# Attention scores over 64 rows instead of 32, odd heads joined by DMA, and a third buffer for VectorE's exponentials

## The chip, the core and the metric

The kernel runs on one core of a Trainium2 chip. A core has five engines that run side by side and meet only at semaphores: TensorE (PE, matrix products into PSUM), ScalarE (ACT, table functions such as the exponential), VectorE (DVE, elementwise work), GpSimd (POOL, used here for a few small jobs) and SyncE (SP, which issues nearly all DMAs of this kernel, strictly in the order in which they were written down). The metric is the time of one execution in device microseconds.

## What is computed

The reference normalises the input and runs two branches on it, an attention block and a token-mixing MLP, and adds both to the input:

```python
xn = _layernorm(x)                       # 2048 tokens x 512
q, k, v = split(xn @ wqkv)               # 32 heads of 16 columns each
p = softmax(q @ k.T * 16 ** -0.5)        # 32 heads x 2048 x 2048
A = (p @ v).reshape(2048, 512) @ wo
u = gelu(layernorm(xn).T @ w1 + b1)      # 512 x 1376, over tokens
B = (u @ w2 + b2).T                      # 2048 x 512
out = x + A + B
```

The softmax dominates: 32 x 2048 x 2048 exponentials. A head has only 16 columns, so a score product uses 16 of the 128 rows of the PE array.

## The kernel before

**Blocks.** Queries are cut into 4 groups of 512 (`qb`). The 32 heads lie in 4 groups of 8 (`T`), and each group is taken in two halves, `e_ = 0` (even heads) and `e_ = 1` (odd heads). A block `b` is one `qb`, one `T` and one `e_`: four heads (`r = 0..3`), 512 queries, all 2048 keys. There are 32 blocks, and each has 16 key tiles `kt` of 128 keys.

**Scores** (`score_mm`, L619). In the transposed keys `KT` and queries `QT`, head `2r` of a group lies on rows 32r to 32r+15 and head `2r+1` on rows 32r+16 to 32r+31. Keys are kept whole. For queries there are two copies per `qb` and `T`, one with the odd heads' rows set to zero and one with the even heads' rows set to zero, made by one VectorE product with a mask (L1032). So a score matmul runs over 32 rows, 16 of which contribute nothing. Two such matmuls (a pair, 128 keys x 512 queries each, into two PSUM banks) are one unit of work. The first pair of a key tile has heads 0 and 1 (rows 0 to 63), the second heads 2 and 3 (rows 64 to 127). Three bank pairs of PSUM rotate.

**Exponentials.** A pair goes either to ScalarE (one `activation`, L696, into a buffer `pT`) or, for up to four key tiles of a block (`D_KTS`), to VectorE, which builds the exponential from bit operations: L880 once per pair out of PSUM, then L899, L906, L912 and L919 once per key tile over all four heads. A key tile treated like this is called a group here. Its intermediate results have two buffers (`dbuf`).

**Weighted values** (`pv_round`, L726). Four matmuls of 128 rows and 32 columns add p times V for four heads into one PSUM bank, head r on partitions 32r to 32r+31: rows 0 to 15 are the result, row 16 is the softmax denominator (V carries a column of ones). A ScalarE tile needs one such round, a VectorE group three.

**End of a block** (`epilogue`). VectorE copies the bank to `OT32` (L811); SP issues four small DMAs that gather the denominators (`rl`), VectorE inverts them (L827), SP puts them to DRAM and spreads them over the partitions again (`denb`); POOL multiplies (L846) into `oT`, which has one slab per block. As odd heads also come out on rows 0 to 15 of their strips, the output weight `wo` is kept in a padded form, `wo_pad`, with eight slabs of 128 rows, half of them zeros, and the output product takes eight matmuls per 128 tokens (L1178, L1205).

**The order.** All instructions are placed by a small planner inside the kernel (`Dispatch`) that runs once when the program is built: it holds an estimated duration for each kind of work (`EST`), steps a clock of its own, and gives every engine its instructions in the order that comes out. On the chip each engine then follows its list in that order and waits at semaphores. The MLP and the projections are filled in as `extras` between scores. The planner also keeps a running sum of PE work over 3.41 us (`GATE_US`) and adds products with a zero matrix (`keep_warm`, L1013) when the sum falls below `GATE_AIM`; a score pair counts as 0.5 in that sum, a full matmul of 512 columns as 1.

## Time and profile before

| what | value |
|---|---|
| median of three runs | 846.33 us (841.46, 846.33, 846.75) |
| the profiled execution | 852.81 us, span 851.0 us |
| mean granted PE clock in the span | 0.954 |
| exponentials on ScalarE | 842 pairs, 783.4 us busy |
| groups on VectorE | 91 (182 pairs) |
| first exponential on ScalarE starts | 14.86 us |
| last one has ended | 839.0 us |

The times are of whole executions; the profile is of one execution, some 6 us longer than the median, and 1.8 us of it lie outside the span. In a line of the profile, the number after `x` is how many instructions the group has, then come busy time and mean duration, and then the engine's idle time just before them with what ended it. Matmul ends are modelled, so a PE that reads as busy may still be running at half speed; the granted clock tells that.

### The profile page before, as it was taken

To read this page: it belongs to the slowest core of one execution; us is meant where nothing else is said; L and a number is where in the kernel's file an instruction comes from. 1 tells how busy PE (TensorE), PEld (TensorE's weight loads), DVE (VectorE), ACT (ScalarE), POOL (GpSimd) and SP (SyncE) were. 2 spreads that over 40 slices of the span, in tenths; PEclk is the share of its full clock that TensorE was granted. 3 is DMA by queue.
4 is the path that set the end of the run, shared out by engine and by line. 5 is a ranking of instruction groups with operands and counts; after the bars stand their busy time and mean duration, and the time that the engine had idled before them with its cause. 6 is when DMAs were issued, how large, how long until landed. Compare 5 with 4: busy or idle time off the path is not lost.

```text
span 851.0 us, 14650 instructions
## 1 busy us (share of the span) xinstructions
PE 783.6 (92%) x6084; PEld 222.4 (26%) x6084; DVE 723.7 (85%) x874; ACT 792.4 (93%) x863; POOL 80.7 (9%) x112
## 2 busy tenths in 40 slices
PE   5999799999999999999999999899899999999995
PEld 3433232222222222222222222212222222222221
DVE  6678788899999899988998989749678999899885
ACT  5999699999999999999999999969889999999994
POOL 5234000000000000000000010000000001000000
PEclk9999799999999999989999999959889999999996
DMA  7100000001111111111001111111020111110000
GB/s 197 27 15 18 22 14 14 8 8 39 40 39 39 39 27 39 38 32 44 22 11 43 43 42 44 43 30 35 21 66 16 25 40 44 43 43 14 15 14 25
DMA packets 75698, 29.25 MB, mean 34 GB/s; under 512 B 63472, under 2 KB 71664, under 8 KB 75632
## 3 DMA queue, kind: packets, MB, share of 16 engines
q1 hardware_dynamic: 72464, 26.75, 12.8%
q10 hardware_dynamic: 3168, 1.57, 0.7%
q8 instruction: 47, 0.77, 0.4%
q14 instruction: 19, 0.16, 0.1%
HBM read 25.70 MB, written 2.35 MB: 33 GB/s over the span
## 4 chain that ended last, share of the span: by engine, by line
ACT 40%; PE 31%; DVE 21%; DMA 3%; SPq 2%; issue 2%; POOL 1%; ACTq 0%; DVEq 0%
ACT pT L696 39%; PE ps L619 12%; PE ps L726 8%; DVE xreg L880 7%; DVE big L906 3%; PE ps L1013 3%; DVE big L912 3%; DVE big L899 2%; DMA rl<-OT 2%; PE ps L1173 2%; DVE xreg L919 2%; SPq L394 1%; PE ps L1178 1%; PE ps L1102 1%; PE ps L1024 1%
## 5 line engine op out<-in xcount | busy, mean ns | idle before, releaser
L696 ACT ACTIVATE pT<-ps 128x1024 bf16<-128x1024 f32 x842 | 783.4, 1114 | 38.0 <-PE ps L619 32.8
L619 PE MATMUL ps<-QT,KT 32*128 32x512 bf16 x2048 | 349.7, 395 | 43.9 <-ACT pT L696 21.8
L880 DVE TENSOR_SCALAR xreg<-ps 128x1024 int16<-128x1024 f32 x182 | 222.2, 1221 | 58.6 <-PE ps L619 57.1
L619 PEld LDWEIGHTS ps<-QT,KT 32*128 32x128 bf16 x2048 | 85.9, 91 | 363.6 <-ACT pT L696 233.6
L726 PE MATMUL ps<-pT,V 128*32 128x512 bf16 x1684 | 160.4, 401 | 2.9 <-DVE V L493 1.5
L906 DVE TENSOR_TENSOR big<-xreg,big 128x2048 bf16<-128x2048 bf16 x91 | 115.9, 1274 | 1.5
L912 DVE TENSOR_TENSOR big<-big 128x2048 bf16<-128x2048 bf16 x91 | 115.3, 1267 | 1.8
L1013 PE MATMUL ps<-xnT,zero 128*128 128x512 bf16 x272 | 83.0, 392 | 0.8 <-DVE OT L811 0.6
L846 POOL TENSOR_TENSOR oT<-OT,denb 128x512 bf16<-128x512 f32 x23 | 35.5, 1545 | 504.5 <-DMA denb<-den_scr 460.3
L899 DVE TENSOR_SCALAR big<-xreg 128x2048 int16<-128x2048 int16 x91 | 66.6, 732 | 1.6
L919 DVE TENSOR_SCALAR xreg<-xreg 128x2048 int16<-128x2048 int16 x91 | 65.5, 720 | 0.0
L726 PE MATMUL ps<-xreg,V 128*32 128x512 bf16 x728 | 58.2, 392 | 4.3 <-DVE xreg L919 4.1
L726 PEld LDWEIGHTS ps<-pT,V 128*32 128x32 bf16 x1684 | 37.8, 95 | 88.9 <-issue 77.4
L1173 PE MATMUL ps<-gT,w2blk 128*128 128x512 bf16 (+1 forms) x176 | 55.4, 392 | 0.2
L1102 PE MATMUL ps<-big,w1blk 128*128 128x512 bf16 (+1 forms) x176 | 53.7, 388 | 0.0
L726 PE MATMUL ps<-big,VS 128*32 128x512 bf16 x364 | 36.1, 387 | 0.0
L846 POOL TENSOR_TENSOR big<-OT,denb 128x512 bf16<-128x512 f32 x8 | 12.6, 1572 | 197.0 <-DMA denb<-den_scr 146.2
L827 DVE RECIPROCAL rl<-rl 128x16 f32<-128x16 f32 x31 | 7.7, 249 | 23.1 <-DMA rl<-OT 23.0
L811 DVE COPY OT<-ps 128x512 f32<-128x512 f32 x31 | 21.2, 685 | 5.1 <-PE ps L726 4.9
L1013 PEld LDWEIGHTS ps<-xnT,zero 128*128 128x128 bf16 x272 | 16.9, 98 | 32.7 <-issue 27.1
L522 PE MATMUL ps<-wqkv_sb,xnT 128*128 128x128 bf16 x256 | 24.6, 227 | 0.0
L726 PEld LDWEIGHTS ps<-xreg,V 128*32 128x32 bf16 x728 | 16.0, 97 | 25.0 <-issue 11.2
(75 smaller groups left out, 365.0 us busy)
## 6 DMA issues: line engine op xcount, KB each, us to landing
denb<-den_scr SPq DMA_DIRECT2D x124, 64.0 KB, 2.0
w1blk<-in_B_w_dram SPq DMA_DIRECT2D x10, 512.0 KB, 4.1
w2blk<-in_B_w_dram SPq DMA_DIRECT2D x16, 320.0 KB, 3.4
big<-in_A_x_dram SPq DMA_DIRECT2D x16, 128.0 KB, 2.1
out_dram<-osb SPq DMA_DIRECT2D x16, 128.0 KB, 1.8
rl<-OT SPq DMA_DIRECT2D x124, 2.0 KB, 1.8
xreg<-in_A_x_dram SPq DMA_DIRECT2D x3, 512.0 KB, 9.0
wqkv_sb<-in_A_wqkv_dram ACTq DMA_DIRECT2D x3, 384.0 KB, 9.9
```

Source lines behind the costliest of these rows:

```text
L619: sc.add("pe", lambda e: e.matmul(bank(bk), lhsT=KT[32 * r:32 * r + 32, T, 128 * kt:128 * (kt + 1)], rhs=QT[32 * r:32 * r + 32, sl, :], st ...
L696: sc.add("act", lambda e: e.activation(pT[:, buf, :], ps[:, s_ * 1024:(s_ + 1) * 1024], ACTF.Exp, scale=EXP_SCALE), reads=[("bank", 2 * s_ ...
L726: sc.add("pe", lambda e, r=r, lhs=lhs, rhs=rhs: e.matmul(bank(PV_BANK)[32 * r:32 * r + 32, :], lhsT=lhs, rhs=rhs, start=first, stop=last, ...
L846: sc.add("pool", lambda e: e.tensor_tensor(oT(qb)[:, G, :], OT32[:, eb, :], denb[:, :], ALU.mult), reads=[("OT32", eb)] + [("denb", r) for ...
L880: sc.add("dve", lambda e: e.tensor_scalar(bv_i[:, i, 1024 * hf:1024 * (hf + 1)], ps[:, s_ * 1024:(s_ + 1) * 1024], EXP_BIAS, 0.0, ALU.add, ...
L899: sc.add("dve", lambda e: e.tensor_scalar(ge_i[:, 0, :], bv_i[:, i, :], 0x7F, 0x3F80, ALU.bitwise_and, ALU.bitwise_or), reads=[("bD", i)], ...
L906: sc.add("dve", lambda e: e.tensor_tensor(ge_f[:, 1 + i, :], bv_f[:, i, :], ge_f[:, 0, :], ALU.mult), reads=[("bD", i), ("gD",)], writes=[ ...
L912: sc.add("dve", lambda e: e.tensor_tensor(ge_f[:, 1 + i, :], ge_f[:, 1 + i, :], ge_f[:, 0, :], ALU.mult), reads=[("eD", i), ("gD",)], writ ...
L919: sc.add("dve", lambda e: e.tensor_scalar(bv_i[:, 2 + i, :], bv_i[:, i, :], 0x7F80, None, ALU.bitwise_and), reads=[("bD", i)], writes=[("v ...
L1013: sc.add("pe", lambda e: e.matmul(bank(PV_BANK), lhsT=zero[:, :], rhs=xnT[:, 0, 0:512], start=first, stop=first), reads=[("zero",)] + [("x ...
L1102: mms = [lambda st=st: sc.add("pe", lambda e: e.matmul(bank(EX_BANK)[0:m, :], lhsT=w1blk[:, slot, st, 0:m], rhs=h_sb[:, st, :], start=(st ...
L1173: mms.append(lambda ft=ft, m=m: sc.add("pe", lambda e: e.matmul(bank(EX_BANK), lhsT=w2blk[0:m, slot, ft, :], rhs=gT[0:m, ft, :], start=(ft ...
```

## The change

1. **Scores over 64 rows.** `QT` has eight slabs instead of four: for each block two versions, and version `r % 2` holds only the 16 rows of heads r = 0 and 2 (or 1 and 3), zeros elsewhere. A score matmul reads 64 rows (0 to 63 or 64 to 127). A pair now has heads r and r+2, so that its two matmuls lie in the two halves of the array. The zero rows are written once by POOL; the 16-row strips come by DMA. VectorE scales the projected queries once into `qst` (512 columns instead of 1024), and SP issues eight DMAs per group of heads (`qt_spread`). The planner counts a score pair as 1.0 (`S_WORK`).
2. **Odd heads on rows 16 to 31.** For odd heads the slice of V starts 16 columns earlier, so that results come out on rows 16 to 31 of the strip and the denominator on row 15. POOL multiplies an odd block into `oTe`, and four DMAs copy its rows 16 to 31 into the even block's slab of `oT`. `wo` needs no padding any more: four matmuls instead of eight per 128 tokens. For the very last block a small padded copy, `wo_last`, remains.
3. **A third buffer** for VectorE's groups (`NDB = 3`, extra space `dmore`).
4. **Planner.** `GATE_AIM` 8.0 to 6.5, with a second test over 0.6 of the stretch; `HOLD_SLACK` 0.3 to 0.2; the gather of denominators is expected to take 3.6 instead of 2.6; POOL's product is put beside a VectorE instruction that reads PSUM (`beside`): it waits for the VectorE instruction ahead of that one, or starts without it after 4 us.
5. Small: the residual rows `xr` move into `w1blk`; padding of V and VS and its memsets go.

```diff
+NDB = 3
-HOLD_SLACK = 0.3
+HOLD_SLACK = 0.2
-GATE_AIM = 8.0
+GATE_AIM = 6.5
+GATE_AIM_SHORT = 6.0
+S_WORK = 1.0
+BESIDE_US = 4.0
...
-        return sum(w for _, w in self.recent) < GATE_AIM
+        if sum(w for _, w in self.recent) < GATE_AIM:
+            return True
+        return sum(w for q, w in self.recent if q >= self.t - 0.6 * GATE_US) < 0.6 * GATE_AIM_SHORT
...
+            sc.add("act", lambda e: e.activation(qst[:, :], bank(EX_BANK), ACTF.Identity, scale=QSCALE),
+                   reads=[("bank", EX_BANK)], writes=[("qst",)])
+            qt_spread(1, 1)
+
+        def qt_spread(sl, e_):
+            for r in range(4):
+                q = 32 * r + 16 * e_
+                dma("sp", QT[q:q + 16, 2 * sl + r % 2, :], qst[q:q + 16, :], reads=[("qst",)],
+                    writes=[("QT", sl, r % 2)], name="qt_spread")
...
-                bank(bk), lhsT=KT[32 * r:32 * r + 32, T, 128 * kt:128 * (kt + 1)],
-                rhs=QT[32 * r:32 * r + 32, sl, :], start=True, stop=True,
-                tile_position=(32 * r, 0)),
+                bank(bk), lhsT=KT[64 * (r // 2):64 * (r // 2) + 64, T, 128 * kt:128 * (kt + 1)],
+                rhs=QT[64 * (r // 2):64 * (r // 2) + 64, 2 * sl + r % 2, :], start=True, stop=True,
+                tile_position=(64 * (r // 2), 0)),
...
-                for r in (2 * hf, 2 * hf + 1):
-                    score_mm(b, kt, r, 2 * s_ + r % 2)
+                for r in (hf, hf + 2):
+                    score_mm(b, kt, r, 2 * s_ + r // 2)
...
-                            return (k * H + 8 * T + 2 * r + e_) * 17
+                            return (k * H + 8 * T + 2 * r + e_) * 17 - 16 * e_
...
-                at[("rl", b)] = dp.use("sp", 4 * EST["sp"]) + EST["dma"]
+                at[("rl", b)] = dp.use("sp", 4 * EST["sp"]) + EST["dma_rl"]
...
+            def mult(after=()):
+                dst = oTe[:, :] if e_ else oT(qb)[:, T, :]
+                keys = [("oTe",)] if e_ else [oT_key(qb, T, 0), oT_key(qb, T, 1)]
...
+            if e_:
+                def put_odd():
+                    for r in range(4):
+                        q = 32 * r + 16
+                        dma("sp", oT(qb)[q:q + 16, T, :], oTe[q:q + 16, :], reads=[("oTe",)],
+                            writes=[oT_key(qb, T, 1)], name="ot_odd")
...
+                if beside and dp.free["pool"] <= dp.t:
+                    beside.pop(0)[1]((sc.streams["dve"][-1],))
...
-                sc.add("dve", lambda e: e.tensor_tensor(
-                    QT[:, 2 * i:2 * i + 2, :], bank(EX_BANK).unsqueeze(1).broadcast_to([128, 2, 512]),
-                    qmask[:, :].unsqueeze(2).broadcast_to([128, 2, 512]), ALU.mult),
+                sc.add("dve", lambda e: e.tensor_scalar(qst[:, :], bank(EX_BANK), QSCALE, None, ALU.mult),
+                       reads=[("bank", EX_BANK)], writes=[("qst",)])
...
+            def go():
+                qt_spread(2 * i, 0)
+                qt_spread(2 * i + 1, 1)
...
-            ng = 0 if lastqb else NG
+            ng = 0 if lastqb else 4
...
-            ng = NG - 2
+            ng = 3
```

## The prediction

> **What bounds the kernel now.** I read the busy shares and the 40 slices first. ScalarE is busy 93% of the span, PE 92%, VectorE 85%; in the row of the granted PE clock some slices fall below 9.

> ```profile
> PE 783.6 (92%) x6084; PEld 222.4 (26%) x6084; DVE 723.7 (85%) x874; ACT 792.4 (93%) x863; POOL 80.7 (9%) x112
> ...
> PEclk9999799999999999989999999959889999999996
> ...
> L696 ACT ACTIVATE pT<-ps 128x1024 bf16<-128x1024 f32 x842 | 783.4, 1114 | 38.0 <-PE ps L619 32.8
> L619 PE MATMUL ps<-QT,KT 32*128 32x512 bf16 x2048 | 349.7, 395 | 43.9 <-ACT pT L696 21.8
> ...
> L1013 PE MATMUL ps<-xnT,zero 128*128 128x512 bf16 x272 | 83.0, 392 | 0.8 <-DVE OT L811 0.6
> ```

> An exponential costs 783.4/842 = 0.930 us of ScalarE. To see where its 58.6 idle us lie I asked for the busy time in stretches (span, PE, PEld, DVE, ACT, POOL, then the clock):

> ```profile
> 80.00:100.00 20.00, 15.15 (x100) 4.28 (x98) 14.11 (x18) 13.30 (x15) 3.34 (x2) 0.66 0.14 41
> 560.00:580.00 20.00, 20.00 (x105) 3.90 (x105) 9.03 (x11) 14.33 (x16) 0.00 (x0) 0.62 0.18 46
> 600.00:620.00 20.00, 17.61 (x125) 4.04 (x125) 15.93 (x18) 15.62 (x17) 1.96 (x1) 0.83 0.05 15
> ...
> 100.00:360.00 260.00, 246.75 (x1984) 69.94 (x1984) 237.55 (x260) 256.99 (x283) 14.73 (x10) 1.00 0.12 28
> ```

> At full clock ScalarE is busy 256.99 of 260 us, 19.77 in 20: it is the bound. In the eight slices of 20 us with a fallen clock (from 80, 360, 380, 540, 560, 600, 620 and 820) it is busy 132.7 us instead of 8 x 19.77 = 158.2. **The clock drops cost 25.5 us.** Start and tail take most of the other idle time.

> **What makes the clock fall.** Followed in steps of 3.41 us, the clock is 1.00 or 0.50, and every change falls on one grid of 3.41 us. Three windows of that grid, the first two followed by a drop, the third not:

> ```profile
> 551.45:554.86 3.41, 2.20 (x20) 0.60 (x16) 3.41 (x3) 3.41 (x5) 0.57 (x1) 1.00 0.00 0
> 599.24:602.65 3.41, 1.32 (x20) 0.37 (x16) 1.85 (x3) 1.91 (x3) 0.00 (x0) 1.00 0.04 3
> 766.49:769.90 3.41, 2.97 (x20) 0.69 (x17) 3.20 (x5) 3.23 (x4) 0.00 (x0) 1.00 0.00 0
> ```

> **What empties those windows** the timelines around the drops show. At 551 POOL's product runs beside VectorE, whose 1.22 us product takes 2.18; the score pair that needs the bank waits, and PE with it:

> ```profile
> 550.27 1.75 POOL L846 TENSOR_TENSOR big<-OT,denb 128x512 bf16<-128x512 f32 x1 [24.36 <-DMA denb<-den_scr]
> 550.93 2.18 DVE L906 TENSOR_TENSOR big<-xreg,big 128x2048 bf16<-128x2048 bf16 x1
> 551.59 0.40 PE L619 MATMUL ps<-QT,KT 32*128 32x512 bf16 x4
> 554.30 0.39 PE L619 MATMUL ps<-QT,KT 32*128 32x512 bf16 x2 [0.65 <-DVE xreg L880]
> ```

> The drops at 377 and 835 look the same. At 603 and 630 a reciprocal stands in VectorE's list before its gather has landed, as SP was still busy with a weight load:

> ```profile
> 591.60 4.61 SPq L395 DMA_DIRECT2D w2blk<-in_B_w_dram  x2
> 596.25 0.43 SPq L395 DMA_DIRECT2D big<-in_A_x_dram  x1
> 596.72 2.41 SPq L394 DMA_DIRECT2D rl<-OT  x4
> 600.31 0.25 DVE L827 RECIPROCAL rl<-rl 128x16 f32<-128x16 f32 x1 [4.95 <-DMA rl<-OT]
> ```

> **The change part by part**, against the span of 851.0 us.

> *Scores over 64 rows.* The same 2048 matmuls of 512 columns. A steady window of 3.41 us has about 9 scores and 12 value matmuls: 0.14 + 0.19 = 0.33 of the array before, 0.28 + 0.19 = 0.47 after, above the limit without any filler. PE's two built lists, with time laid along the score pairs at the trace's pace (0.92 us each in the first 128, 0.79 later), agree: 7.7% of windows of 3.41 us lie under 0.37 before, 2.5% after. I keep that third of the loss: -25.5 + 8.2 = **-17.3 us**. Bounds: 0 (the stalls empty PE whatever the weights) to -25.5.

> *PE's time.* The new list has 74 zero matmuls instead of 272 and 60 fewer with `wo`: -258 x 0.215 = -55 us. Five more groups add ten rounds, +2. What is lost is the overlap of one pair's rows 0 to 63 with the next pair's 64 to 127: the four scores above ran in 0.40 us, where two pairs one after the other show 0.61. The old list has 288 such places, of which 81 started together: +17 us, bounds 0 and 288 x 0.215 = 62. Net -36 us (+9 at worst), worth nothing by itself, as ScalarE has 1.2% of idle time in clean stretches. The trace has no 64-row matmul; the nearest row is the 32-row pair, two side by side in 0.39.

> [...]

> *Ten exponentials fewer on ScalarE.* The new list has 832 pairs there and 96 groups on VectorE: -10 x 0.930 = **-9.3 us**. VectorE gets 5 x (2 x 1.221 + 0.732 + 1.274 + 1.267 + 0.720) = 32.2 us. It loses 15 x (1.216 - 0.69) = 7.9 with the queries' evacuation, and, if POOL's product lies beside L880 as planned, the stretching: the four long operations average 1274, 1267, 732 and 720 ns where undisturbed ones show 1224, 1224, 690 and 685, 91 x 0.165 = 15 us. So 733 us in a span near 823, 89%: cover enough, since stretches with 95% run at full ScalarE speed. If POOL starts elsewhere, the 15 us come back on VectorE; in clean stretches ScalarE hardly feels them, but one more drop costs it 2 to 9 us (the slices above).

> *Start.* ScalarE writes `qst` before its first exponential, and must wait for VectorE's read of that bank, which ends at 15.23; 0.69 us for `qst` and 0.27 for a key copy follow, so the first exponential comes near 16.3 instead of 14.86: **+1.5**. POOL's memset of 3072 columns at 1.93/2192 a column is 2.7 instead of 1.9 us; its successors wait for the input's DMA (landed at 8.89) anyway, 0 to +0.5, taken as 0.

> *SP.* New are 124 strips of queries and 60 strips of odd heads. Strips with one buffer key wait for each other's landing; 1.8 to 2.0 us is the nearest rows' time to landing (`rl`, `denb`). A spread of eight then holds SP for 2 x (1.9 + 0.8) = 5.4 us, a join of four for 3 x 1.9 + 0.4 = 6.1: 11.5 per two blocks of some 26 us each, where SP now idles over half the time. Queued behind them are gathers, puts and weight loads; only a late gather is felt, by VectorE's reciprocal. Between copy and reciprocal VectorE's new list holds 4.0 to 6.3 us of work (median 4.9; before 1.4 to 6.4, median 3.8), and a gather on time needs 2.41 + 1.8 = 4.2. In SP's list, loads or a spread stand close ahead of the gathers of blocks 20 to 23 and 25: 2.6, 3.2, 2.2, 5.8 and 0.6 us late, 14 us of VectorE's idle time against the 23.0 that its waits show now. Taken as -2 on ScalarE; bounds -5 and +45, all joins and spreads half in the way. Query strips have half a block, 13 us, before their first use.

> *The rest* (third buffer, `xr`, one evacuation fewer per key) changes no count on ScalarE: 0. The tail keeps its steps, 12 us from the last exponential.

> **Sum:** 851.0 - 17.3 - 9.3 + 1.5 - 2 = 824 us of span, with the 1.8 outside **825.5 us**. That is 2.5% under the median of 846.33, though 3.2% under the execution it is made against; the median runs may have lost some 6 us less to the clock.

> **Rivals.** (1) *The drops stay*, because stalls make them, not thin windows: -9.3 + 1.5 gives 843 + 1.8 = 845, no change. For it: five of seven drops stand behind a named stall. Against: the same stalls elsewhere left no drop where filler stood beside. 0.15. (2) *Slower: SP's list.* If the strips land in 4 us instead of 1.9 (the longest gather took 4.9), a join holds SP for 12 us and a spread for 10; from the point where 20 of the 31 gathers come 3 us late or more, VectorE idles 60 us in order, PE's fixed list waits behind it, and the 1.2% of slack is gone: 825 + 60 less the 14 counted, 870. 0.08. (3) *Zero rows don't count for the clock*, while the filler is gone: 21% of the new list's windows would be under the limit instead of 7.7%, 25.5 x 21/7.7 = 70 us of loss, 851 - 9.3 + 1.5 + 44 + 1.8 = 889. Against: the zero matrices of L1013 do count in the fit. 0.04. (4) *64-row halves don't run side by side*: 1024 x 0.215 = 220 us more PE, then the bound, over 900. 0.02. Better than 812 (no drop left, fewer stalls): 0.05. The forecast, 812 to 836: 0.66.

> **Numbers.** A measurement of this kernel tells about 1% from no change (838 to 855). Faster: 0.66 + 0.05 + 0.02 of the first rival = 0.73; same 0.13; slower 0.14. A range of 808 to 846 holds 0.8.

> **What would show it.** Right: a clock near 0.98 with two or three drops, 832 exponentials at 0.93 us, L906 and L912 near 1230 ns, score pairs at 0.39. Wrong: long VectorE idle times ended by the gather's DMA, joins of over 6 us on SP, scores of two pairs at 0.43 apart, or as many slices of fallen clock as before.

## The result and the profile after

The changed kernel takes 839.32 us (median of 20 runs, 836.08 to 843.60), the kernel before, measured beside it, 850.61 us (20 runs, 841.46 to 857.07). The ratio is 0.9892, with a 95% interval of 0.9867 to 0.9916: **1.1% faster, where 2.5% were forecast.** The profiled execution after took 837.79 us, with a span of 835.7 us and a mean granted PE clock of 0.984 (before 0.954). Executions of one kernel differ in their mean granted clock (0.947 to 0.980 before, 0.976 to 0.986 after): the ratios here leave out the longest ones, medians in us count all, and the profiled execution of the kernel before (852.81 us, clock 0.954, where most others of it have 0.96 to 0.98) is one of the longer, so the two profiles differ by 15.3 us where the ratio stands for 9.

From the page of the kernel after, the busy line, the row of the granted clock and three of the costliest groups (line, engine, operation, tiles and shapes, count | busy us, mean ns | idle us just before them, with what ended most of it):

```profile
PE 734.9 (88%) x5866; PEld 212.3 (25%) x5866; DVE 730.1 (87%) x900; ACT 783.0 (94%) x854; POOL 74.1 (9%) x110
...
PEclk9999999999999999999989999999999999999998
...
L720 ACT ACTIVATE pT<-ps 128x1024 bf16<-128x1024 f32 x832 | 773.3, 1151 | 29.9 <-PE ps L643 25.8
L643 PE MATMUL ps<-QT,KT 64*128 64x512 bf16 x2048 | 367.6, 388 | 68.9 <-ACT pT L720 29.9
...
L1059 PE MATMUL ps<-xnT,zero 128*128 128x512 bf16 x74 | 21.8, 388 | 0.2 <-ACT KT L506 0.2
```

L720 is the old L696, L643 the old L619, L1059 the old L1013. The stretches that had a fallen clock before, and the clean one (stretch, length, then busy time and instructions of PE, PEld, DVE, ACT and POOL, then the clock, the DMA share and GB/s), of the kernel after:

```profile
80.00:100.00 20.00, 18.10 (x164) 6.23 (x164) 19.33 (x23) 20.00 (x23) 1.26 (x1) 1.00 0.07 18
560.00:580.00 20.00, 15.92 (x128) 4.36 (x127) 16.17 (x18) 17.73 (x21) 1.86 (x1) 1.00 0.10 23
600.00:620.00 20.00, 17.97 (x145) 4.94 (x148) 17.25 (x20) 19.58 (x22) 0.00 (x0) 1.00 0.21 48
100.00:360.00 260.00, 238.91 (x1916) 66.94 (x1912) 240.07 (x272) 253.22 (x278) 13.51 (x10) 0.99 0.15 32
```

The clock is back: counted in steps of 3.41 us, it was at half speed for 79.7 us before and is for 29.5 us now, in six single steps and the tail. But look at the last line: between 100 and 360 us ScalarE is busy 253.22 us, **less** than the 256.99 us before, and only 1.4 us of that are lost in a half-speed step (at 262 us); in the second line it lacks 2 us at a full clock. Something new holds it up.

The span can be closed on ScalarE alone, from the group lines and the start of the first exponential:

| us | before | after | change | forecast |
|---|---|---|---|---|
| exponentials (842, 832) | 783.4 | 773.3 | -10.1 | -9.3 |
| its waits ahead of them | 38.0 | 29.9 | -8.1 | -19.3 (clock -17.3, SP -2) |
| first exponential starts | 14.86 | 17.09 | +2.2 | +1.5 |
| span | 851.0 | 835.7 | -15.3 | -27 |

The first three changes add up to -16.0, so hardly anything is left over. Eleven of the missing twelve microseconds are waits of ScalarE. Summed over the half-speed steps between its first and last exponential, ScalarE is idle for 66.6 - 44.8 = 21.8 us before and 20.5 - 13.1 = 7.4 us after. So its waits inside the drops fell by 14.4 us (forecast 17.3), and its waits outside them rose from 16.2 to 22.5 us, by 6.3, where a fall of 2 was forecast.

**What the waits are.** The whole timeline of all engines around 515 us, of the kernel after (start, length, engine, line, operation, tiles, count; in brackets the idle time before it and what ended it; SPq is SP's queue of DMA issues, a run of equal issues being one piece):

```profile
509.63 4.08 SPq L416 DMA_DIRECT2D w2blk<-in_B_w_dram  x2
...
513.76 0.43 SPq L416 DMA_DIRECT2D w1blk<-in_A_x_dram  x1
...
514.23 6.07 SPq L416 DMA_DIRECT2D QT<-qst  x8
...
517.98 0.39 PE L643 MATMUL ps<-QT,KT 64*128 64x512 bf16 x2 [3.01 <-DMA QT<-qst]
...
518.41 1.22 DVE L926 TENSOR_SCALAR xreg<-ps 128x1024 int16<-128x1024 f32 x1 [2.97 <-PE ps L643]
```

SP is in a weight load for 4.08 us, so the eight query strips start only at 514.23. The next block's first score needs strips r = 0 and r = 2. The second was issued only when the first had landed, so PE stands idle for 3.01 us, VectorE for 2.97. The 3.41 us grid shows the price:

```profile
514.99:518.40 3.41, 0.42 (x6) 0.23 (x6) 0.45 (x1) 2.01 (x3) 0.00 (x0) 1.00 0.19 53
518.40:521.81 3.41, 3.41 (x20) 0.65 (x20) 3.37 (x3) 1.88 (x2) 0.00 (x0) 0.50 0.11 22
521.81:525.22 3.41, 3.41 (x46) 0.98 (x38) 1.60 (x3) 3.37 (x5) 0.00 (x0) 1.00 0.28 61
```

The emptied window is followed by one at clock 0.50, and ScalarE loses about 1.4 us in each of the two. The same chain (weight load of 4.00 us, spread of 5.94, PE waiting 2.10) stands before the drop at 723. The join of odd heads does the same to the output product, once:

```profile
792.33 5.87 SPq L416 DMA_DIRECT2D oT<-oTe  x4
...
799.47 0.39 PE L1255 MATMUL ps<-wo_sb,oT 128*128 128x512 bf16 x1 [2.15 <-DMA oT<-oTe]
```

Most other stalls end at SP as well: VectorE's reciprocal waits 2.3 to 3.7 us for a late gather at 260, 413, 563 and 588 us, and three of these lead to a drop in the next window. The gather at 260 was issued behind a join that had held SP for 7.51 us, the other three behind a weight load. Of the six drops only the one at 429.7 stands behind no wait on SP: there POOL's product of 1.27 us (from 423.12) lies beside a VectorE product that takes 2.30 us instead of 1.22, and PE then waits 1.18 us for VectorE. SP's own waits in the kernel after (engine, line, what for: us in total, times, longest) say what holds it, beside waits for inputs that it would have in any order:

```profile
SPq L416 <- DMA w2blk<-in_B_w_dram: 51.2, 16, 3.5
...
SPq L416 <- DMA oT<-oTe: 47.5, 33, 2.9
...
SPq L416 <- DMA QT<-qst: 24.2, 36, 2.3
```

In all three SP waits for a DMA that it has issued itself, whose bytes the next DMA doesn't touch. The kernel tracks dependencies by buffer keys; the two strips of a slab of `QT`, the four strips of odd heads in one slab of `oT`, and the two parts of one load of `w2blk` each share a key, so the later write waits for the earlier one's landing. The first two are new, the third (49.6 us) was there before.

### The profile page after: what moved, and what is told of

Its sections match the earlier page's. It is cut to its first block, busy times and chain, and to the rows that moved or that the text cites. A ratio compares the mean times of both kernels' runs of the same rounds, so it can differ in the third digit from the quotient of the medians.

```text
span 835.7 us, 14448 instructions
## 1 busy us (share of the span) xinstructions
PE 734.9 (88%) x5866; PEld 212.3 (25%) x5866; DVE 730.1 (87%) x900; ACT 783.0 (94%) x854; POOL 74.1 (9%) x110
## 4 chain that ended last, share of the span: by engine, by line
ACT 45%; PE 25%; DVE 17%; DMA 8%; SPq 2%; issue 2%; POOL 1%; ACTq 0%; DVEq 0%
ACT pT L720 45%; PE ps L643 11%; DVE xreg L926 8%; PE ps L744 7%; PE ps L1152 3%; PE ps L1223 2%; DMA w2blk<-in_B_w_dram 2%; DVE big L952 2%; DMA QT<-qst 2%; DMA oT<-oTe 2%; DVE big L958 2%; DMA rl<-OT 1%; SPq L415 1%; DVE big L945 1%; SPq L416 1%
## 5 line engine op out<-in xcount | busy, mean ns | idle before, releaser
L720 ACT ACTIVATE pT<-ps 128x1024 bf16<-128x1024 f32 x832 | 773.3, 1151 | 29.9 <-PE ps L643 25.8
L643 PE MATMUL ps<-QT,KT 64*128 64x512 bf16 x2048 | 367.6, 388 | 68.9 <-ACT pT L720 29.9
L926 DVE TENSOR_SCALAR xreg<-ps 128x1024 int16<-128x1024 f32 x192 | 234.7, 1223 | 61.0 <-PE ps L643 55.9
L643 PEld LDWEIGHTS ps<-QT,KT 64*128 64x128 bf16 x2048 | 90.1, 93 | 359.8 <-ACT pT L720 218.5
L744 PE MATMUL ps<-xreg,V 128*32 128x512 bf16 x512 | 46.7, 395 | 0.8 <-DVE xreg L965 0.8
L876 POOL TENSOR_TENSOR oTe<-OT,denb 128x512 bf16<-128x512 f32 x15 | 19.0, 1268 | 302.2 <-DVE big L958 151.9
L876 POOL TENSOR_TENSOR oT<-OT,denb 128x512 bf16<-128x512 f32 x12 | 17.8, 1482 | 296.8 <-DMA denb<-den_scr 274.0
L965 DVE TENSOR_SCALAR dmore<-xreg 128x2048 int16<-128x2048 int16 x64 | 43.7, 683 | 0.0
L744 PE MATMUL ps<-dmore,V 128*32 128x512 bf16 x256 | 26.0, 396 | 7.2 <-DVE dmore L965 7.2
L965 DVE TENSOR_SCALAR xreg<-xreg 128x2048 int16<-128x2048 int16 x32 | 22.1, 692 | 0.0
L1059 PE MATMUL ps<-xnT,zero 128*128 128x512 bf16 x74 | 21.8, 388 | 0.2 <-ACT KT L506 0.2
L849 DVE RECIPROCAL rl<-rl 128x16 f32<-128x16 f32 x31 | 7.6, 246 | 14.9 <-DMA rl<-OT 14.9
## 6 DMA issues: line engine op xcount, KB each, us to landing
xreg<-in_A_x_dram SPq DMA_DIRECT2D x3, 512.0 KB, 10.1
```

Of the source, the lines that this page charges most:

```text
L643: sc.add("pe", lambda e: e.matmul(bank(bk), lhsT=KT[64 * (r // 2):64 * (r // 2) + 64, T, 128 * kt:128 * (kt + 1)], rhs=QT[64 * (r // 2):64 ...
L720: sc.add("act", lambda e: e.activation(pT[:, buf, :], ps[:, s_ * 1024:(s_ + 1) * 1024], ACTF.Exp, scale=EXP_SCALE), reads=[("bank", 2 * s_ ...
L744: sc.add("pe", lambda e, r=r, lhs=lhs, rhs=rhs: e.matmul(bank(PV_BANK)[32 * r:32 * r + 32, :], lhsT=lhs, rhs=rhs, start=first, stop=last, ...
L876: sc.add("pool", lambda e: e.tensor_tensor(dst, OT32[:, eb, :], denb[:, :], ALU.mult), reads=[("OT32", eb)] + [("denb", r) for r in range(4)],
L926: sc.add("dve", lambda e: e.tensor_scalar(bv_i[:, i, 1024 * hf:1024 * (hf + 1)], ps[:, s_ * 1024:(s_ + 1) * 1024], EXP_BIAS, 0.0, ALU.add, ...
L965: sc.add("dve", lambda e: e.tensor_scalar(vp_i(i), bv_i[:, i, :], 0x7F80, None, ALU.bitwise_and), reads=[("bD", i)], writes=[("vD", i)] + ...
```

## The experiments

Each ratio is against the kernel before, measured beside it on the same chip; the before's median there was 843.6 to 847.9 us. "Waits" is the idle time ahead of ScalarE's exponentials in the profiled execution (38.0 before, 29.9 after).

### The SP queue: a key for each strip

```diff
-writes=[("QT", sl, r % 2)], name="qt_spread"
+writes=[("QT", sl, r % 2, r)], name="qt_spread"
-writes=[oT_key(qb, T, 1)], name="ot_odd"
+writes=[oT_key(qb, T, 1 + r)], name="ot_odd"
```

Each score matmul reads only its own strip's key; the readers of `oT` list all five. The order on every engine is that of the changed kernel.

> The changed kernel with a buffer key of its own for each strip of queries and for each strip of odd heads, so that SP no longer waits for one strip's landing before it issues the next; every engine's order stays. Theory 'SP's list': in the changed kernel's trace, ScalarE loses some 25 us around waits that end with SP (query strips landing late 6.7 us on PE, gathers 14.9 us on VectorE, a join 2.2 us). A spread then holds SP for 8 x 0.45 = 3.6 instead of 6.0 us, a join for 4 x 0.5 = 2.0 instead of 5.9: 825 to 831 us, the clock's drops 2 or 3 instead of 7. Rival 'planned order': the stalls come from the order itself, SP is merely the last to be late: within 3 us of the changed kernel's 839. Rival 'clock': drops as before in number, time within 3 us of 839.

**826.15 us, ratio 0.9759 (0.969 to 0.9829).** That is 11 us below the changed kernel by the ratios, 13 by the medians, 11.7 by the spans (824.0 against 835.7). Waits fell from 29.9 to 21.0. The timeline of this kernel at the same block change:

```profile
507.11 4.96 SPq L416 DMA_DIRECT2D QT<-qst  x8
...
510.13 0.39 PE L643 MATMUL ps<-QT,KT 64*128 64x512 bf16 x1 [0.62 <-DMA QT<-qst]
...
516.26 0.61 PE L643 MATMUL ps<-QT,KT 64*128 64x512 bf16 x4
```

A spread now holds SP for 4.96 us instead of 6.07. More important, PE waits 0.62 us instead of 3.01: strip 2 no longer starts behind strip 0's landing. All PE's waits for strips fall from 6.7 us to 2.8.

The two halves of this edit alone, first the queries, then the joins:

> The changed kernel with keys of their own for the query strips alone (joins of odd heads as in the changed kernel). Theory 'spreads': the query strips are what SP is held by at the wrong place (6.0 us each, 15 times; PE waited 6.7 us for them, and gathers and puts queue behind them): 827 to 832 us. Rival 'joins': 837 to 840 us, and the gain is in the other half.

**830.80 us, ratio 0.9835 (0.9776 to 0.9893)**, waits 25.0.

> The changed kernel with keys of their own for the strips of the odd heads' joins alone. Theory 'spreads': 834 to 839 us, as a join stands after its block's gather and mostly has 10 us of room, but for the wait of 2.2 us at 799. Rival 'joins': 827 to 831 us.

**833.49 us, ratio 0.9869 (0.98 to 0.9939)**, waits 23.9. Their waits lie 4.9 and 6.0 us under the changed kernel's 29.9, and above the 21.0 of both halves together. By the ratios the queries' half is some 5 us faster than the changed kernel and the joins' half 2, both inside the intervals: how the 11 to 13 us divide is not settled.

### The weight load with the same fault

```diff
-reads=[], writes=[("w2blk", slot)], name="ld_w2b"
+reads=[], writes=[("w2blkb", slot)], name="ld_w2b"
```

The product with the last part of `w2` reads the new key. Done on top of the previous kernel, and alone on the kernel before:

> The kernel of e1_own_keys, and in addition the two parts of each weight load w2 have a key of their own, so that SP doesn't wait 3.4 us for the landing of the first before it issues the second; same order. Theory 'SP's list': three of the five long VectorE waits left (gathers 3 to 4 us late at 409, 555 and 582) stand behind such a load; they go, and the clock's drops with them: 815 to 821 us. Rival 'DMA shared': the gather's landing, not its issue, is late, since the weight load of 320 KB moves at the same time: within 3 us of 826.

**809.81 us, ratio 0.958 (0.9525 to 0.9636): the fastest kernel of this study, 4.2% under the kernel before.** Its costliest group and SP's timeline, of this kernel:

```profile
L720 ACT ACTIVATE pT<-ps 128x1024 bf16<-128x1024 f32 x832 | 769.2, 1171 | 6.7 <-PE ps L643 3.4
```

```profile
498.95 1.18 SPq L416 DMA_DIRECT2D w2blk<-in_B_w_dram  x2
500.19 0.42 SPq L416 DMA_DIRECT2D w1blk<-in_A_x_dram  x1
500.65 4.97 SPq L416 DMA_DIRECT2D QT<-qst  x8
...
532.07 2.43 SPq L416 DMA_DIRECT2D big<-oTe  x4
```

The weight load holds SP for 1.18 us instead of 4.08, a join 2.43 instead of 5.87. The waits ahead of exponentials are 6.7 us, the clock is 0.996 and falls only in the tail; VectorE waits 2.7 us in all for gathers (12.7 with the strips' keys alone).

> The kernel before with the two parts of each weight load w2 on keys of their own; same order. Theory 'SP's list': the waits of 4.95 and 2.24 us ahead of VectorE's reciprocal go, and with them the drops at 603 and 630: 6 to 12 us under the kernel before. Rival 'DMA shared': no change, within 3 us.

**834.49 us, ratio 0.9895 (0.9812 to 0.9978).** On the kernel before, this one key is worth 9 us (2 to 16 by the interval), about as much as the whole change brought. On top of the strips' keys it was worth 15 to 16.

### What the rows are worth, and what the lost overlap costs

First the changed kernel with its scores on the head's own 32 rows (the zero rows left out of the product, the same result):

```diff
-lhsT=KT[64 * (r // 2):64 * (r // 2) + 64, ...], tile_position=(64 * (r // 2), 0)
+lhsT=KT[32 * r:32 * r + 32, ...], tile_position=(32 * r, 0)
```

> The changed kernel, same order, but each score matmul runs over its own 32 rows only (the zero strips are left out; the result is the same). Theory 'area': the clock goes by the share of the array in use, so without the doubled rows a fifth of the windows of 3.41 us come under the limit: mean clock under 0.90, 870 to 910 us. Rival 'stalls alone': the rows don't count for the clock, it falls where PE is held up; mean clock about 0.98, 839 us within 4. Rival 'overlap': rows of neighbouring pairs now differ (0 and 64 against 32 and 96), so that neighbouring pairs run together again, and PE gains up to 50 us of slack: 833 to 838.

**880.54 us (four executions, 864.13 to 893.86), ratio 1.0255 (1.012 to 1.039).** The clock row and costliest group of this kernel, in an execution of 888.41 us:

```profile
PEclk9599997896999998899889898799888959879975
...
L720 ACT ACTIVATE pT<-ps 128x1024 bf16<-128x1024 f32 x832 | 780.8, 1114 | 71.5 <-PE ps L643 65.6
```

In the new order, with 74 filler products instead of 272, the zero rows are worth 31 us by the ratios. Nothing but the rows differs; their new place would, by the author's estimate, let neighbouring pairs overlap again, as in the kernel before (four scores in 0.40 us at 551), which speaks for the 32 rows and doesn't make up for the clock. The clock is at half speed for 221.7 us in this execution instead of 29.5; in the shortest, of 864.13 us, its mean of 0.910 stands for an estimated 155 us (twice 0.090 of the span). So rows of zeros count for the clock here (mean 0.984 with them, 0.876 without, in the profiled executions), which agrees with the author's estimate that it goes by the share of the array in use.

Then the kernel before with 64 rows in the scores, its order and filler kept:

```diff
-lhsT=KT[32 * r:32 * r + 32, ...], tile_position=(32 * r, 0)
+lhsT=KT[64 * (r % 2):64 * (r % 2) + 64, ...], tile_position=(64 * (r % 2), 0)
```

> The kernel before, same order and same filler, but each score matmul runs over 64 rows (0 to 63 for heads 0 and 2, 64 to 127 for heads 1 and 3); the scores then add up two heads' products and the values are not the reference's, only the work is of the same size. Theory 'area': a steady window rises by 0.14 of the array, nearly all drops go: mean clock 0.99, 851 - 20 = 828 to 834 us. Rival 'stalls alone': drops stay as they are, 850 us within 4. Rival 'lost overlap': neighbouring pairs no longer run together, 81 x 0.215 = 17 us of PE time come back, and eat part of it: 836 to 845.

**843.68 us, ratio 0.9984 (0.9945 to 1.0023): no measurable change**, although the clock rose to 0.989. The rows bring the clock and take something else. The next kernel takes that alone: 32 rows as before, but the second pair of a key tile in the same rows as the first, so that neighbouring pairs can't overlap.

```diff
-lhsT=KT[32 * r:32 * r + 32, ...], tile_position=(32 * r, 0)
+lhsT=KT[32 * (r % 2):32 * (r % 2) + 32, ...], tile_position=(32 * (r % 2), 0)
```

> The kernel before, same order, still 32 rows a score, but heads 2 and 3 use the rows of heads 0 and 1 (their own keys and queries are left out, so the values are not the reference's), so that a pair can no longer run beside the pair before it. Theory 'overlap has a price': 81 places x 0.215 = 17 us more PE time; some windows get thinner at their ends, 3 to 10 us over the kernel before. That would explain why 64 rows in the order before took away the drops and gave only some 4 us. Rival 'slack': PE has room, within 3 us of the kernel before.

**861.60 us, ratio 1.0165 (1.008 to 1.0251): the lost overlap costs 14 us** (7 to 21 by the interval; 3 to 10 were expected). PE is busy with scores for 373.0 us, before for 349.7. The two groups, of the kernel with 32 rows and no overlap, and of the kernel before with 64 rows:

```profile
L696 ACT ACTIVATE pT<-ps 128x1024 bf16<-128x1024 f32 x842 | 785.8, 1088 | 41.2 <-PE ps L619 35.1
```

```profile
L696 ACT ACTIVATE pT<-ps 128x1024 bf16<-128x1024 f32 x842 | 784.8, 1087 | 24.7 <-PE ps L619 18.1
```

These two have the same order, filler and lack of overlap, and differ in the rows alone: waits fall by 16.5 us, half-clock time from 80.2 us to two short drops and the tail, and the time by 15 us (ratios). That is about the forecast's -17.3, in the order before and with the overlap gone on both sides.

### POOL's wait, the start, the third buffer

The changed kernel, and then the fastest one, without POOL's wait for a VectorE instruction:

```diff
-beside.pop(0)[1]((sc.streams["dve"][-1],))
+beside.pop(0)[1]()
```

> The changed kernel, same order, but POOL's product no longer waits for the VectorE instruction ahead of the one that reads PSUM: it starts as soon as its own inputs are there. Theory 'port': products again fall beside VectorE's long SBUF operations; their stretching goes from about 8 us in the changed kernel to 15 to 20 us, the time up by 2 to 8 us, one or two drops more. Rival 'no matter': the wait only moves POOL's product, ScalarE has other causes to wait: within 2 us of 839.

> The kernel of e5_own_keys_w2 without POOL's wait for the VectorE instruction ahead, as in e4_pool_no_wait. Theory 'port': VectorE's long operations are stretched by some 8 us more in all, 2 to 6 us slower, 812 to 816. Rival 'no matter': within 2 us of 809.8, as in e4_pool_no_wait.

**835.16 us, ratio 0.9868 (0.9791 to 0.9945), and 812.73 us, 0.9598 (0.955 to 0.9646): no difference from the kernels with the wait** (0.9892 and 0.958). The wait does shift POOL's work. The two long VectorE products, after and without the wait:

```profile
L952 DVE TENSOR_TENSOR big<-xreg,big 128x2048 bf16<-128x2048 bf16 x96 | 120.0, 1250 | 0.2
L958 DVE TENSOR_TENSOR big<-big 128x2048 bf16<-128x2048 bf16 x96 | 118.3, 1233 | 1.9
```

```profile
L958 DVE TENSOR_TENSOR big<-big 128x2048 bf16<-128x2048 bf16 x96 | 122.3, 1274 | 1.9
L952 DVE TENSOR_TENSOR big<-xreg,big 128x2048 bf16<-128x2048 bf16 x96 | 121.5, 1266 | 0.2
```

Without the wait VectorE is stretched by some 5.5 us more in these two lines (96 x 16 ns and 96 x 41 ns). The time shows none of it.

The start, in the fastest kernel, with `qst` written by VectorE instead of ScalarE:

```diff
-sc.add("act", lambda e: e.activation(qst[:, :], bank(EX_BANK), ACTF.Identity, scale=QSCALE),
+sc.add("dve", lambda e: e.tensor_scalar(qst[:, :], bank(EX_BANK), QSCALE, None, ALU.mult),
```

> The kernel of e5_own_keys_w2 with the first scaled copy of the queries (qst) written by VectorE instead of ScalarE at the start, so that ScalarE doesn't wait for VectorE's read of the bank before its first exponential. Theory 'start': the first exponential comes 1.3 to 1.5 us earlier (15.0 instead of 16.4), the whole 1 to 1.5 us faster: 808.5. Rival 'hidden': the first scores set it, no change.

**812.55 us, ratio 0.9579 (0.9523 to 0.9634): no gain in time.** The first exponential starts at 16.37 us, against 16.35 with ScalarE's copy. But the two profiled executions didn't reach this point at the same time. ScalarE's first copy of the queries and its first exponential, of the fastest kernel and then of the one with VectorE's `qst`:

```profile
14.12 0.69 ACT L564 ACTIVATE QT<-ps,qmask 128x512 bf16<-128x512 f32 x1 [0.21 <-PE ps L558]
...
16.35 3.03 ACT L720 ACTIVATE pT<-ps 128x1024 bf16<-128x1024 f32 x3
```

```profile
15.20 0.69 ACT L564 ACTIVATE QT<-ps,qmask 128x512 bf16<-128x512 f32 x1 [0.17 <-PE ps L558]
...
16.37 1.02 ACT L720 ACTIVATE pT<-ps 128x1024 bf16<-128x1024 f32 x1 [0.32 <-PE ps L643]
```

From the one to the other it is 2.23 us with ScalarE's `qst` and 1.17 with VectorE's, as in the kernel before (13.69 to 14.86). So the edit does take away 1.06 us, but everything ahead ran 1.08 us later in that execution, where VectorE waited 1.48 us for a part of the input (0.60 in the other). A gain of 1 us is below what four executions of 807.25 to 813.84 us can show.

Two buffers instead of three, in the fastest kernel (`NDB = 2`; the planner then makes another order, with 846 exponentials on ScalarE and 89 groups on VectorE):

> The kernel of e5_own_keys_w2 with two buffers for VectorE's groups instead of three; the planner then gives VectorE fewer groups, and the order differs. Theory 'third buffer lets VectorE take more': 7 groups fewer on VectorE, 14 pairs more on ScalarE, 14 x 0.93 = 13 us slower, 820 to 826. Rival 'count unimportant': within 4 us of 809.8.

**823.48 us, ratio 0.9719 (0.9672 to 0.9765)**, 10.9 us over the 812.55 of the kernel with VectorE's start, which ran on the same chip. The costliest group of the kernel with two buffers:

```profile
L720 ACT ACTIVATE pT<-ps 128x1024 bf16<-128x1024 f32 x846 | 782.7, 1180 | 7.6 <-PE ps L643 5.9
```

Waits are as low as with three buffers (7.6 against 6.7); the difference is 782.7 - 769.2 = 13.5 us of exponentials. Once little else holds ScalarE, most of what a pair costs there shows in the time.

## Why the prediction was wrong, step by step

**The step that failed is the term for SP, "taken as -2 on ScalarE".** In its place the shared keys cost 11 to 13 us, and ScalarE's waits outside the drops grew by 6.3 us. The forecast made SP's list a gain; it was a loss. Typical hold times were right: 5.9 to 7.7 us for a spread, median 6.1 (forecast 5.4), 5.8 to 7.5 for a join, median 5.9 (6.1), and strips landed in 1.8 us in the median. The sum for gathers was right too, in part by luck: VectorE waited 14.9 us for them, forecast 14, before 23.0. In blocks 20 to 22 it was 8.1 us (forecast 8.0); the 6.4 us forecast for blocks 23 and 25 didn't come, and 5.9 us came in blocks 8 and 14, where none were forecast. Wrong was the sentence "only a late gather is felt", and with it "Query strips have half a block, 13 us, before their first use". In the stall shown above, `qst` was written at 511.0 us and its strips were needed at about 515. SP's list was walked for the gathers, but not for the strips, where a weight load stood ahead of the spread. The waits are from the kernel after:

```profile
DVE rl L849 <- DMA rl<-OT: 14.9, 8, 3.7
...
PE ps L643 <- DMA QT<-qst: 6.7, 4, 3.0
```

The waits of 3.01 and 2.10 us on PE for a strip emptied their windows directly (PE was busy for 0.42 of 3.41 us in the first), and the clock fell to 0.50 on top, at 518 and 723 us; late gathers did the same three times by way of VectorE. The prediction had SP's list as its second rival, tied to strips that land in 4 us. Its warning sign, joins of over 6 us, did come: five of the fifteen joins held SP for 6.8 to 7.5 us, where one strip each took 2.7 to 3.4 us to land. But most strips landed in 1.8 us, and the loss came at a quarter of the rival's price.

**Clock drops, -17.3: right in the main**, -14.4 us of ScalarE's waits between the two profiles, and 15 us between the kernels with 64 and 32 rows and no overlap. The limit of about 0.37 of the array in a window of 3.41 us, an estimate from the trace before, held within a few hundredths: weighted in the same way, the windows ahead of drops in the kernel after have 0.06 to 0.36, and none at 0.38 or above is followed by one; with 32 rows in the new order drops go up to 0.40. What the forecast had only as a bound is that a stall of some 3 us empties a window with 64 rows too (PE busy for 0.42 of 3.41 us at 515, 0.39 of 3.40 at 413), so the third that was to remain came as six drops instead of two or three, each one window long.

**The lost overlap, part of a term "worth nothing by itself": wrong in the old order**, 14 us. It was priced on PE, at 17 us of matmul time under 36 us of net relief. How it reaches ScalarE is shown only in part. In the two profiled executions, both at clock 0.954, ScalarE's waits are 3.2 us longer without the overlap (41.2 against 38.0) and the span 6.1 (857.1 against 851.0). Beyond that the clock is lower, which fits the rest without showing the chain: 0.936 to 0.962 in the four executions without the overlap, 0.960 to 0.976 in the seven of the kernel before measured beside them. In the new order 258 fewer matmuls go against it. With the strips' keys waits are 21.0 us there, where the old order without overlap and with 64 rows has 24.7. That this is the relief was not measured by itself.

**Ten exponentials, -9.3: right** (-10.1), and the two-buffer kernel shows the price once more. **Cover on VectorE: right**; it has 87% of the span, and stretching it by 5.5 us changed nothing. **Start, +1.5: right in cause**, and somewhat large: ScalarE's wait and `qst` add 1.06 us between the copy of the queries and the first exponential (2.23 us in the kernels after, 1.17 before and with VectorE's `qst`). The rest of the measured +2.2 is a later input: the copy itself began at 14.86 us, before at 13.69. **Tail, 0: right**, 11.5 us from the last exponential against 11.1 before (the last one before ended at 839.9 us, not 839.0). The terms of the sum add up to 825.7, not 825.5, which changes nothing.

**The other rivals.** *The drops stay* fell: 79.7 to 29.5 us of half speed in the profiles, and a clock of 0.976 to 0.986 in the twenty executions after, against 0.947 to 0.980 in those of the kernel before. *Zero rows don't count* fell with the 31 us of the 32-row kernel. *64-row halves don't run side by side* fell: a pair reads 0.39 us, and two pairs 0.61 (the last line shown of the kernel with own keys), so each pair streams in an estimated 0.22. A weight load for a score takes 93 ns in the kernel after; at 0.22 us from pair to pair no time for one is seen between them.

The forecast's 825.5 stands beside the 826.15 of the kernel with own keys. This is close partly by chance: that kernel still has 12.7 us of late gathers, and the weight load's share was in the forecast's base without being known.

## What to carry to other kernels

In a queue that issues in order, price every transfer by how long it holds the queue and by what stands behind it **and** ahead of it, for each consumer, up to the moment at which that consumer needs it. Look in the queue's own waits for a wait on a transfer that it has issued itself: if the two write different bytes, the dependency is only in the bookkeeping, and a key for each part removes it. A gain on the clock was to be had here from the share of the array in use per window of 3.41 us (mean clock 0.954 with 32 rows and 0.989 with 64, where order, filler and lack of overlap were the same); it is to be checked against the overlap that the larger tiles give up, here 14 us in the order before.

## What was not expected of the hardware

- Two score pairs on different rows overlapping is worth 14 us of 847 in the kernel before (7 to 21 by the interval), although ScalarE was its bound. The 81 places at which they started together stand for 17 us of matmul time; that the two numbers are near each other explains nothing by itself.
- One fallen window didn't always lead to more. With fuller windows every drop ahead of the tail in the profile after was a single step of 3.41 us (in the kernel with the strips' own keys one was two steps); before, drops lasted up to 20.5 us.
- The time that the issuing queue spends waiting on its own transfers was worth 11 to 13 us for the strips and 15 to 16 for the weight load, of some 830. Starting the DMAs held SP even where none waited for another: 4.96 us for eight strips in the kernel with own keys, 0.62 each, beside 1.8 from issue to landing in the kernel after.
